# Sums of a GLU unit's first pair in a timed chain, a set's last sums and stores behind it, and other steps for decoding

## The chip, the cores and the metric

One core of one Trainium2 chip runs the whole program. The metric is the device time of one execution in microseconds (us), as the median of several runs. The engines are TensorE (PE, with its weight loads as PEld), VectorE (DVE), ScalarE (ACT), GpSimd (POOL) and SyncE (SP), which issues all DMAs of this kernel.

## What is computed

```python
# attention within chunks of 64 tokens; B, H, S, D = 4, 8, 576, 64
attn = softmax(q_c @ k_c.T / sqrt(D)); x = (attn @ v_c) -> [2304, 512]
# mixture of 4 experts, all of them used, F = 1024
p = domain_probs / domain_probs.sum(-1)
x = sum over e of p[:, e] * (relu(x @ w1[e]) @ w2[e])
# RMSnorm and GLU, F = 1536
xn = x / sqrt(mean(x * x) + 1e-6) * rms_g
out = (silu(xn @ w_gate) * (xn @ w_val)) @ w_out
```

The GLU weights arrive as 64-bit floats and are turned into 32-bit floats on the chip ("decoding").

## The kernel before, in words

**Products.** A 32-bit operand is split into a high part (rounded by a cast on ACT) and a low part (the remainder, a subtraction, mostly on POOL), and a product is three passes of high by high, high by low and low by high. Large products use Strassen's scheme: 7 products in place of 8, with sums of operands before and sums of results after.

**Tiling.** The 2304 tokens are 3 sets of 6 tiles of 128, a set has two blocks of 384 tokens. The program goes through MoE sets 0, 1 and 2 (in the trace about 50 to 800 us, behind an opening piece of attention) and then GLU sets 0, 1 and 2 (801 to 960, 960 to 1117, 1117 to 1282). Attention for set s+1 runs beside MoE set s.

**A GLU unit.** A set has three units (index `k`), a unit two pairs of columns of F (index `fp`). For each pair `hidden` (L766) runs twice, for gate and then for value: seven products a, b, d, c, a, d, c of 6 matmuls each into PSUM tiles `a_ps`, `b_ps`, `c_ps`, `d_ps` (L721). The first product is copied out by ACT (`p`, L774) and the second `a_ps` product may only start after that copy. `gate_use` takes ACT's sigmoid (`sg`, L829) and multiplies on DVE; `val_use` (L850) multiplies by the value (L856), which gives `silu` tiles, and then forms the operand sums `h_s3`, `h_s1`, `h_s2` of the next Strassen product: on POOL for the unit's first pair, on DVE for its second (`late`). `part` (L843) makes the high part of each by a cast on ACT (`hh`, L846) and returns the function that makes the low part on POOL (`hl`).

**The unit's output product.** `outer_strassen` (L926) then multiplies by w_out: seven products (L950) in the order 0, 6, 4, 5, 1, 3, 2, each added by `take` into eight accumulators `out_u2`, `out_c..`, `out_y..`. In a set's last unit (`end`) six closing sums (four on POOL, two on DVE) and the stores of the results (`write`, DMA at L981) stand between these products.

**What sets the order.** The program is written out by one Python pass; each engine executes its instructions in the order in which they were emitted. Beside the main loop stand background generators, the chains of class `Chains` (L73): after each emitted product `work.tick(us)` advances a clock of estimated microseconds, and each chain whose due time has come is stepped; `every` (and `busy` within hidden products) is the spacing of its steps, `pause` a wait on that clock, `force` runs a chain to its end. Chains load weights (`w1_load`, DMA at L298 from `wgv`; w_out by L375 from `wou`, 4 buffers), run attention (`at` = e/sum on POOL, L616, before the transposes `trA` of PE, L526), decode (`decode`, L393; six DVE operations per tile, L405 to L419, and an addition on POOL) and form and store Strassen's weight sums (`prepare`, L429; `store_q`, DMA at L454). Decoding and preparing run from MoE set 1 on:

```python
decode(): every 1.15, busy=3.5;  prepare(): every 1.0
```

A wait at the head of an engine's queue holds up everything behind it, SP's DMA issues included.

Of the kernel before, what the change touches and what calls it, by code (L numbers as in the profile page):

```python
# [18 lines left out]
P = 128  # L19
# [53 lines left out]
class Chains:  # L73
# [78 lines left out]
def fused_kernel(ctx, tc, qkv, probs, w12, wglu, gvec, out):  # L152
# [4 lines left out]
    nc = tc.nc  # L157
# [12 lines left out]
    NB = TPB * P  # L170
# [6 lines left out]
    tp = Slots(tc, ctx, "tp", 32, [P, 512], F32)  # L177
    cp = Slots(tc, ctx, "cp", 8, [P, NB], F32)
# [9 lines left out]
    work = Chains()  # L188
# [11 lines left out]
    sub = lambda eng, o, a, b: eng.tensor_tensor(o, a, b, op=ALU.subtract)  # L200
    add = lambda eng, o, a, b: eng.tensor_tensor(o, a, b, op=ALU.add)  # L201
# [529 lines left out]
    def catch_up():  # L731
        while later:
            later.pop(0)()
# [107 lines left out]
    plain_h, parted = {}, {}  # L841

    def part(fp, n, src):  # L843

        hi, lo = hh.get("hh"), hl.get("hl")
        nc.scalar.copy(hi, src)  # L846
        parted[fp, n] = (hi, lo)
        return lambda: sub(nc.gpsimd, lo, src, hi.bitcast(F32))

    def val_use(fp, late):  # L850
        eng = nc.vector if late else nc.gpsimd

        def use(b, j, ps):
            m = silu.pop((b, j))
            v = m[:, :NB]
            nc.vector.tensor_tensor(v, ps[:, :NB], v, op=ALU.mult)  # L856
            banks.put(ps)
            plain_h[fp, b, j] = m
            at = lambda *bj: plain_h[(fp, *bj)][:, :NB]
            if (b, j) == (1, 1):  # L860
                later.append(part(fp, 0, v))
            elif (b, j) == (0, 1):
                s3, s1 = cp.get("h_s3"), cp.get("h_s1")
                sub(eng, s3, at(1, 1), v)
                add(eng, s1, v, at(0, 0))
                tp.put(plain_h.pop((fp, 0, 1)))
                plain_h[fp, "s1"] = s1
                los = [part(fp, 6, s3), part(fp, 4, s1)]

                def rest():  # L870
                    for lo in los:
                        lo()
                    cp.put(s3)

                later.append(rest)
            elif (b, j) == (1, 0):
                s1, s2 = plain_h.pop((fp, "s1")), cp.get("h_s2")
                sub(eng, s2, s1, at(1, 1))
                cp.put(s1)
                tp.put(plain_h.pop((fp, 1, 1)))  # L880
                lo = part(fp, 5, s2)

                def rest():
                    lo()
                    sub(nc.gpsimd, s2, v, s2)
                    plain_h[fp, "s4"] = s2

                later.append(rest)

        return use  # L890

    acc = {}
# [30 lines left out]
        w2p.put(*w2)  # L923


    def outer_strassen(s, u, fps, end, aside):  # L926

        catch_up()
        w = 2 * P
        if u == 0:  # L930
            for n in ("u2", "c22", "y1", "c11", "c21", "y2", "c12", "y3"):
                acc[n] = tp.get(f"out_{n}")
        spots = {0: (0, 0), 6: (1, 0), 4: (2, 1), 5: (3, 1)}
        big, small, opened = {}, {}, set()

        def mult(n, place, by_tile=False):
            half, y = spots[place]
            half = (0, 1, 1, 0)[half]
            if place not in big:
                big[place] = bank(f"x_{place}")  # L940
                if y not in small:
                    small[y] = bank(f"y_{y}")
            wt = weight(("w2", "glu", s, u, n))
            wv = wt.rearrange("p k (a n) -> p k a n", a=2)
            order = [(q, t) for q in range(UF) for t in range(TPB)]
            for q, t in sorted(order, key=lambda o: o[1]) if by_tile else order:
                ps = big[place] if t < 2 else small[y]
                o = (t if t < 2 else half) * w
                for m, (hx, wi) in enumerate(PASSES):
                    nc.tensor.matmul(  # L950
                        ps[:, o:o + w], parted[fps[q], n][hx][:, t * P:(t + 1) * P], wv[:, q, wi],
                        start=id(ps) not in opened, stop=(n in (1, 2, 3, 5) and (q, m) == (UF - 1, len(PASSES) - 1)),
                        skip_group_check=True,
                    )
                    opened.add(id(ps))
                work.tick(3 * 0.12)
            w2p.put(wt)
            for fp in fps:
                hi, lo = parted.pop((fp, n))
                hh.put(hi)  # L960
                hl.put(lo)

        def take(o, ps, cols=slice(None), first=u == 0):
            if first:
                nc.scalar.copy(acc[o][:, cols], ps[:, cols])
            else:
                add(nc.vector, acc[o][:, cols], ps[:, cols], acc[o][:, cols])
# [7 lines left out]
        low, high = slice(0, w), slice(w, 2 * w)  # L975

        def write(o, cols, b, d, ts):
            i = s * TPS + b * TPB
            for n, t in enumerate(ts):
                c = slice(cols.start + n * w, cols.start + (n + 1) * w)  # L980
                nc.sync.dma_start(out=out[(i + t) * P:(i + t + 1) * P, d * w:(d + 1) * w], in_=acc[o][:, c])  # L981

        mult(0, 0)
        take("u2", big[0])
        more(1, 1, 0)
        aside(0)
        mult(6, 6)
        take("c22", big[6])
        take("y1", small[0])
        more(3, 0, 0)  # L990
        aside(1)
        mult(4, 4)
        take("c22", big[4], first=False)
        more(2, "s4")
        aside(2)
        mult(5, 5)
        take("u2", big[5], first=False)
        take("y1", small[1], first=False)
        banks.put(big[5])
        aside(3)  # L1000
        if end:
            for eng, o, cols, x in (
                (nc.gpsimd, "c21", slice(0, 512), "u2"), (nc.gpsimd, "y2", high, "y1"),
                (nc.vector, "c12", slice(0, 512), "u2"), (nc.vector, "y3", high, "y1"),
                (nc.gpsimd, "c22", slice(0, 512), "u2"), (nc.gpsimd, "y1", high, "y1"),
            ):
                src = acc[x][:, low if x == "y1" else cols]
                add(eng, acc[o][:, cols], acc[o][:, cols], src)
            write("c22", slice(0, 512), 0, 1, (0, 1))
            write("y1", high, 0, 1, (2,))  # L1010
        mult(1, 0)
        take("c11", big[0])
        banks.put(big[0])
        aside(4)
        if end:
            write("c11", slice(0, 512), 1, 0, (0, 1))
        mult(3, 6)
        take("c21", big[6])
        take("y2", small[0])
        banks.put(big[6], small[0])  # L1020
        aside(5)
        if end:
            write("c21", slice(0, 512), 0, 0, (0, 1))
            write("y2", low, 1, 0, (2,))
            write("y2", high, 0, 0, (2,))
        mult(2, 4, True)
        take("c12", big[4])
        take("y3", small[1], high)
        banks.put(big[4], small[1])
        aside(6)  # L1030
        if end:
            write("c12", slice(0, 512), 1, 1, (0, 1))
            write("y3", high, 1, 1, (2,))
            for n in ("u2", "c22", "y1", "c11", "c21", "y2", "c12", "y3"):
                tp.put(acc.pop(n))


    def norm(s):
# [79 lines left out]
    with tc.manual_schedule():  # L1118
# [72 lines left out]
        for kind, s in [(kind, s) for kind in ("moe", "glu") for s in range(NSET)]:  # L1191
            moe = kind == "moe"
            final = not moe and s == NSET - 1
# [5 lines left out]
            for k, (e, fps) in enumerate(plan):  # L1199
                end = k == len(plan) - 1  # L1200
# [8 lines left out]
                    feeding[1] = feeding[3] = 0.8  # L1209
                if moe and s == 1 and k == 0:  # L1210
                    work.add(fetch64())
                    work.add(decode(), 1.15, busy=3.5)
                    work.add(prepare(), 1.0)
                if k == len(plan) - 2 and not final:
                    if ahead is None:
                        ahead = work.add(turn(0 if moe else s + 1), 1.0)
# [40 lines left out]
                if moe:  # L1257
                    outer(fps, w2, flush, aside)
                else:
                    outer_strassen(s, k, fps, end, aside)  # L1260
        work.force(None, lambda: not work.chains)


# [57 lines left out]
```

## Time and profile before

| what | value |
|---|---|
| median of 3 runs | 1280.35 us (1276.58 to 1282.26) |
| profiled execution | 1284.08 us |
| its span | 1282.3 us |
| mean granted TensorE clock | 0.984 of full |
| PE / PEld busy | 1218.4 us (95%) / 1130.6 us (88%) |
| DVE busy | 831.6 us (65%) |
| POOL busy | 714.5 us (56%) |
| ACT busy | 487.5 us (38%) |
| DMA, mean over the span | 233 GB/s |

Busy time of an engine is the time in which one of its instructions runs; PE's 95% leaves about 64 us of the span in which it does nothing. "Granted clock" is the share of full speed that TensorE is given in a stretch: at 0.5 it runs at 1.2 instead of 2.4 GHz and a product takes twice as long while it still counts as busy, so PE's lost time is more than its idle time.

### The profile page before, as it was taken

The page shows a single profiled execution, that of the slowest core. Times are in us where ns is not written, and L with a number is a line of the kernel's source. Part 1 is how long each engine was busy: PE and PEld are TensorE (multiplying, and loading weights), DVE is VectorE, ACT ScalarE, POOL GpSimd, SP SyncE. Part 2 cuts the span into 40 slices and gives each one's busy share as a digit, 9 for nine tenths or more (in the row PEclk, how much of TensorE's full clock was granted, in tenths as well). Part 3 has the DMA queues.
Part 4 walks back from the last instruction along what each step waited for, and adds up shares of the span by engine and source line. Part 5 has one row for each costly group of instructions (what it writes and reads, how often), then busy time and mean ns, then how long its engine had stood idle before and what let it go on. Part 6 is the DMA issues. An engine that isn't in the chain of part 4 may idle for free.

```text
span 1282.3 us, 22321 instructions
## 1 busy us (share of the span) xinstructions
PE 1218.4 (95%) x7740; PEld 1130.6 (88%) x7740; DVE 831.6 (65%) x1450; ACT 487.5 (38%) x1164; POOL 714.5 (56%) x763
## 2 busy tenths in 40 slices
PE   7999999999999999999999999999987999979997
PEld 6878899989999888899899998999986999879997
DVE  5755544475787877887877777645664466644655
ACT  6545433342262344242443333344451432413311
POOL 4797666652575755576755665352464334643434
PEclk9999999999999999999999999999999999989999
DMA  8478555555787997667897786467748658396583
GB/s 266 150 273 276 170 174 195 182 191 197 238 286 261 318 306 246 218 241 254 280 297 273 273 285 245 145 221 264 262 149 276 217 182 288 123 318 204 185 297 115
DMA packets 152898, 299.34 MB, mean 233 GB/s; under 512 B 17745, under 2 KB 22353, under 8 KB 152785
## 3 DMA queue, kind: packets, MB, share of 16 engines
q1 hardware_dynamic: 152784, 297.90, 68.7%
q8 instruction: 62, 1.02, 0.3%
q14 instruction: 52, 0.42, 0.1%
HBM read 227.58 MB, written 70.25 MB: 232 GB/s over the span
## 4 chain that ended last, share of the span: by engine, by line
PE 78%; POOL 9%; DVE 3%; issue 3%; DMA 3%; ACT 2%; SPq 1%; POOLq 0%; DVEq 0%; ACTq 0%
PE o L908 28%; PE d_ps L721 11%; PE a_ps L721 11%; PE c_ps L721 11%; PE x L950 6%; PE b_ps L721 5%; PE y L950 3%; POOL w L200 2%; POOL hl L200 2%; POOL tw L200 1%; DMA w<-wgv 1%; DMA w1m<-w 1%; PE pv L553 1%; POOL h_s L200 1%; POOL at L616 1%
## 5 line engine op out<-in xcount | busy, mean ns | idle before, releaser
L908 PE MATMUL o<-w,hh 128*128 128x512 f32 x1152 | 357.8, 392 | 0.6 <-POOL w L200 0.6
L908 PEld LDWEIGHTS o<-w,hh 128*128 128x128 f32 x1152 | 215.4, 188 | 44.4 <-POOL w L200 1.4
L200 POOL TENSOR_TENSOR w<-r,w 128x512 fp32r<-128x512 f32 (+1 forms) x146 | 164.5, 1135 | 116.0 <-ACT w L360 50.0
L721 PE MATMUL c_ps<-x,w 128*128 128x384 f32 x1080 | 222.3, 344 | 4.2 <-DVE d_ps L201 3.3
L908 PE MATMUL o<-w,hl 128*128 128x512 f32 x576 | 224.8, 390 | 0.0
L721 PE MATMUL a_ps<-x,w 128*128 128x384 f32 x984 | 203.4, 343 | 19.1 <-ACT p L774 19.0
L721 PE MATMUL d_ps<-x,w 128*128 128x384 f32 x984 | 204.6, 345 | 11.9 <-DMA w<-wgv 11.9
L721 PEld LDWEIGHTS c_ps<-x,w 128*128 128x128 f32 x1080 | 193.8, 193 | 6.3 <-DVE d_ps L201 4.7
L721 PEld LDWEIGHTS a_ps<-x,w 128*128 128x128 f32 x984 | 175.3, 192 | 25.4 <-ACT p L774 22.7
L721 PEld LDWEIGHTS d_ps<-x,w 128*128 128x128 f32 x984 | 178.2, 194 | 12.7 <-issue 12.5
L200 POOL TENSOR_TENSOR hl<-silu,hh 128x384 fp32r<-128x384 f32 x54 | 56.6, 1071 | 234.0 <-ACT hh L846 234.0
L1244 DVE SCALAR_TENSOR_TENSOR acc<-o,pr,acc 128x512 f32<-128x512 f32 x126 | 94.3, 749 | 130.9 <-PE o L908 130.8
L908 PEld LDWEIGHTS o<-w,hl 128*128 128x128 f32 x576 | 108.4, 188 | 22.8
L201 POOL TENSOR_TENSOR w<-w,sc 128x512 f32<-128x512 f32 x36 | 46.8, 1299 | 138.2 <-DVE sc L419 131.0
L200 POOL TENSOR_TENSOR w<-tw,w 128x256 fp32r<-128x256 f32 x136 | 112.4, 836 | 4.5 <-ACT w L235 4.5
L201 DVE TENSOR_TENSOR u<-b_ps,p 128x384 f32<-128x384 f32 x82 | 45.4, 554 | 100.3 <-ACT p L774 60.7
L235 ACT CAST w<-tw 128x256 fp32r<-128x256 f32 x136 | 51.7, 406 | 135.0 <-POOL tw L200 131.7
L721 PE MATMUL b_ps<-x,w 128*128 128x384 f32 x492 | 98.7, 336 | 0.0
L950 PE MATMUL x<-w,hh 128*128 128x256 f32 x504 | 95.9, 283 | 0.0
L811 ACT ACTIVATE hh<-d_ps 128x384 fp32r<-128x384 f32 x92 | 45.2, 492 | 127.9 <-DVE d_ps L201 127.9
L200 POOL TENSOR_TENSOR hl<-h_s,hh 128x384 fp32r<-128x384 f32 x72 | 76.8, 1087 | 20.5 <-ACT hh L846 20.5
L774 ACT COPY p<-a_ps 128x384 f32<-128x384 f32 x82 | 39.3, 479 | 126.2 <-PE a_ps L721 126.0
(135 smaller groups left out, 1961.4 us busy)
## 6 DMA issues: line engine op xcount, KB each, us to landing
w<-wgv SPq DMA_DIRECT2D x252, 256.0 KB, 4.5
w<-w1m SPq DMA_DIRECT2D x224, 256.0 KB, 5.3
r<-in_w SPq DMA_DIRECT2D x128, 256.0 KB, 5.0
w<-wou SPq DMA_DIRECT2D x63, 512.0 KB, 6.1
w1m<-w SPq DMA_DIRECT2D x112, 256.0 KB, 2.7
wgv<-w SPq DMA_DIRECT2D x84, 256.0 KB, 4.8
raw<-in_wglu SPq DMA_DIRECT2D x36, 512.0 KB, 4.1
wou<-w SPq DMA_DIRECT2D x42, 256.0 KB, 4.4
```

What stands on the lines that cost most here:

```text
L200: sub = lambda eng, o, a, b: eng.tensor_tensor(o, a, b, op=ALU.subtract)
L201: add = lambda eng, o, a, b: eng.tensor_tensor(o, a, b, op=ALU.add)
L235: nc.scalar.copy(halves(out[n])[:, 0], at[part_of[n]])
L553: nc.tensor.matmul(ps[n][lo:lo + CH, o:o + CH], vt[a][row:row + CH, hp, c, :], aT[a][row:row + CH, q:q + CH], start=True, stop=True,)
L616: nc.gpsimd.tensor_tensor(t.rearrange("p (hp r n) -> p hp r n", hp=HP, r=2)[:, :, h2 ^ a, :], rows(e)[:, a * HP:(a + 1) * HP, :], rs[:, a ...
L721: nc.tensor.matmul(ps[:, :NB], wv[:, wi, k, :], xs[n][:, xi, k, :], start=(first and k == 0 and m == 0), stop=(last and k == KH - 1 and m ...
L774: nc.scalar.copy(p1, v(a))
L811: nc.scalar.activation(hi, src, AF.Relu)
L908: nc.tensor.matmul(ps, hs[fps[k], b, j][hx][:, r * P:(r + 1) * P], w2[2 * k + j][:, wi], start=((k, j, m) == (0, 0, 0)), stop=((k, j, m) = ...
L950: nc.tensor.matmul(ps[:, o:o + w], parted[fps[q], n][hx][:, t * P:(t + 1) * P], wv[:, q, wi], start=id(ps) not in opened, stop=(n in (1, 2 ...
L1244: nc.vector.scalar_tensor_tensor(out=acc[i], in0=ps, scalar=pr[:, i, e:e + 1], in1=acc[i], op0=ALU.mult, op1=ALU.add,)
```

## The change

The core of the diff; `outer_strassen` is now called `second`, and L numbers move by it.

```diff
+    def sums_ahead(fp):
+        at = lambda *bj: plain_h[(fp, *bj)][:, :NB]
+        s3, s1 = cp.get("h_s3"), cp.get("h_s1")
+        sub(nc.gpsimd, s3, at(1, 1), at(0, 1))
+        add(nc.gpsimd, s1, at(0, 1), at(0, 0))
+        tp.put(plain_h.pop((fp, 0, 1)))
+        yield from work.pause(2.8)
+        los = [part(fp, 6, s3), part(fp, 4, s1)]
+        yield from work.pause(1.2)
+        for lo in los:
+            lo()
+        cp.put(s3)
+        while (fp, 1, 0) not in plain_h:
+            yield
+        s2 = cp.get("h_s2")
+        sub(nc.gpsimd, s2, s1, at(1, 1))
...
+        yield from work.pause(1.6)
+        lo = part(fp, 5, s2)
+        yield from work.pause(0.8)
+        lo()
+        sub(nc.gpsimd, s2, at(1, 0), s2)
...
     def val_use(fp, late):
...
+            elif not late:
+                if (b, j) == (0, 1):
+                    summed.append(work.add(sums_ahead(fp)))
...
+    def second(s, u, fps, end, final, aside):
+        for c in summed:
+            if c in work.chains:
+                work.force(c, lambda: c not in work.chains)
...
+        def finish():
+            yield from work.pause(4)
+            for o, y in (("c21", "y2"), ("c12", "y3"), ("c22", "y1")):
+                plus(nc.gpsimd, o)
+                yield from work.pause(1.5)
+                plus(nc.gpsimd, y, high)
+                yield from work.pause(1.5)
+            for args in (
+                ("c11", both, 1, 0, (0, 1)), ("c21", both, 0, 0, (0, 1)), ("c12", both, 1, 1, (0, 1)),
+                ("c22", both, 0, 1, (0, 1)), ("y2", low, 1, 0, (2,)), ("y2", high, 0, 0, (2,)),
+                ("y3", high, 1, 1, (2,)), ("y1", high, 0, 1, (2,)),
+            ):
+                write(*args)
+                yield from work.pause(1)
+            yield from work.pause(5)
+            tp.put(*ac.values())
...
-        if end:
+        if final and end:
...
-            write("c22", slice(0, 512), 0, 1, (0, 1))
-            write("y1", high, 0, 1, (2,))
...
             write("y2", high, 0, 0, (2,))
+            write("c22", both, 0, 1, (0, 1))
+            write("y1", high, 0, 1, (2,))
...
+        elif end:
+            work.add(finish())
...
-                    work.add(decode(), 1.15, busy=3.5)
-                    work.add(prepare(), 1.0)
+                    decoding, preparing = work.add(decode(), 1.15, busy=3.5), work.add(prepare(), 1.0)
+                if moe and (s, k) in ((1, 4), (2, 0)):
+                    decoding[1], decoding[3], preparing[1] = (1.7, 5.0, 1.5) if s == 1 else (1.05, 3.2, 0.9)
```

In words: (1) The sums of a unit's first pair, which were emitted at once inside the value product, are emitted by a chain `sums_ahead` with pauses between sum, cast and remainder; `second` forces the chain to its end before it begins. (2) At the end of GLU sets 0 and 1 the six closing sums, now all on POOL, and the twelve stores are emitted by a chain `finish` behind the unit, beside the next set's first unit, and the eight accumulators stay taken until then. In the last set only the order of the stores changes: those of c22 and y1 stand behind those of c11, c21 and y2. (3) From step 4 of MoE set 1 decoding and preparing take wider steps (1.7, 5.0 and 1.5), and from the start of MoE set 2 closer ones than before (1.05, 3.2 and 0.9).

PE's order of instructions is the same in both kernels. What stands on other engines moves, and the decoding that ended in MoE set 2's last step now ends in GLU set 0's first unit: two tiles' decoding on DVE, about ten POOL operations, casts on ACT and the last seven stores of L454 stand there, two of these stores ahead of the last two w_out loads of that unit.

**ACT, GLU set 0, first unit: end of the first pair's value product and start of the second pair's gate product** (`COPY p` is L774, `hh` the high parts). Before:

```order
L774 COPY p_9891<-a_ps 128x384
L846 CAST hh<-silu 128x384
L846 CAST hh<-h_s_9951 128x384
L846 CAST hh<-h_s_9952 128x384
L846 CAST hh<-h_s_9973 128x384
L774 COPY p_9987<-a_ps 128x384
L829 ACTIVATE sg<-d_ps 128x384
L829 ACTIVATE sg<-a_ps 128x384
L829 ACTIVATE sg<-d_ps 128x384
L829 ACTIVATE sg<-c_ps 128x384
L774 COPY p_10070<-a_ps 128x384
```

Now:

```order
L774 COPY p_9853<-a_ps 128x384
L846 CAST hh<-silu 128x384
L774 COPY p_9938<-a_ps 128x384
L846 CAST hh<-h_s_9923 128x384
L846 CAST hh<-h_s_9924 128x384
L829 ACTIVATE sg<-d_ps 128x384
L829 ACTIVATE sg<-a_ps 128x384
L829 ACTIVATE sg<-d_ps 128x384
L846 CAST hh<-h_s_9994 128x384
L829 ACTIVATE sg<-c_ps 128x384
L774 COPY p_10040<-a_ps 128x384
```

The copy `p` of the next hidden product stands ahead of the two casts of sums, and the third cast stands behind three `sg`.

**SP, end of GLU set 0** (`wgv` are the loads of the next set's first products, `out` the stores). Before:

```order
L375 DMA w_11470<-wou_137 128x1024
L298 DMA w_0_11478<-wgv_0_107 128x512
L298 DMA w_5_11486<-wgv_0_107 128x512
L981 DMA out<-out_c_10148 128x256 x2
L981 DMA out<-out_y_10149 128x256
L298 DMA w_4_11510<-wgv_0_107 128x512
L298 DMA w_6_11521<-wgv_0_107 128x512
L981 DMA out<-out_c_10150 128x256 x2
L298 DMA w_1_11535<-wgv_0_107 128x512
L298 DMA w_2_11543<-wgv_0_107 128x512
L298 DMA w_3_11551<-wgv_0_107 128x512
L981 DMA out<-out_c_10151 128x256 x2
```

Now:

```order
L375 DMA w_11470<-wou_137 128x1024
L298 DMA w_0_11478<-wgv_0_107 128x512
L298 DMA w_5_11486<-wgv_0_107 128x512
L298 DMA w_4_11501<-wgv_0_107 128x512
L298 DMA w_6_11512<-wgv_0_107 128x512
L298 DMA w_1_11524<-wgv_0_107 128x512
L298 DMA w_2_11532<-wgv_0_107 128x512
L298 DMA w_3_11540<-wgv_0_107 128x512
L298 DMA w_0_11555<-wgv_1_108 128x512
L298 DMA w_5_11566<-wgv_1_108 128x512
L298 DMA w_4_11574<-wgv_1_108 128x512
L298 DMA w_6_11588<-wgv_1_108 128x512
```

No store stands between the loads of the next set's first products.

**DVE, end of MoE set 1** (L405 to L419 decode; `s_0`, `s_1` are operand sums of the next set; `u`, `v`, `d_ps` the result sums of the running product). Before:

```order
L405 TENSOR_SCALAR w_6563<-raw 128x512
L1244 SCALAR_TENSOR_TENSOR acc_4079<-o_6556,pr,acc_4079 128x512
L409 SCALAR_TENSOR_TENSOR w_6563<-raw,w_6563 128x512
L413 TENSOR_SCALAR sc<-raw 128x512
L201 TENSOR_TENSOR s_0_6591<-xr 128x384
L200 TENSOR_TENSOR s_0_6593<-s_0_6591,xr 128x384
L201 TENSOR_TENSOR u_6610<-b_ps,p_6596 128x384
L201 TENSOR_TENSOR s_1_6592<-xr 128x384
L201 TENSOR_TENSOR v_6625<-d_ps,u_6610 128x384
L415 SCALAR_TENSOR_TENSOR w_6563<-sc,w_6563 128x512
L200 TENSOR_TENSOR s_1_6594<-s_1_6592,xr 128x384
L200 TENSOR_TENSOR s_0_6637<-xr 128x384
```

Now:

```order
L1304 SCALAR_TENSOR_TENSOR acc_4079<-o_6481,pr,acc_4079 128x512
L419 SCALAR_TENSOR_TENSOR sc<-raw,sc 128x512
L201 TENSOR_TENSOR s_0_6518<-xr 128x384
L200 TENSOR_TENSOR s_0_6520<-s_0_6518,xr 128x384
L201 TENSOR_TENSOR u_6538<-b_ps,p_6523 128x384
L201 TENSOR_TENSOR s_1_6519<-xr 128x384
L201 TENSOR_TENSOR v_6552<-d_ps,u_6538 128x384
L200 TENSOR_TENSOR s_1_6521<-s_1_6519,xr 128x384
L200 TENSOR_TENSOR s_0_6564<-xr 128x384
L201 TENSOR_TENSOR d_ps<-c_ps,v_6552 128x384
```

L405, L409 and L413 of one more tile no longer stand ahead of the sums, nor L415 between `v` and `d_ps`.

## Rows read from the trace of the kernel before

**Rows 1.** The page, part 4: the chain that ended last, by engine.
```profile
PE 78%; POOL 9%; DVE 3%; issue 3%; DMA 3%; ACT 2%; SPq 1%; POOLq 0%; DVEq 0%; ACTq 0%
```

**Rows 2.** Waits of PE, 801 to 1282 us: us in total, times, longest us.
```profile
PE a_ps L721 <- ACT p L774: 17.0, 9, 2.0
PE d_ps L721 <- DMA w<-wgv: 11.9, 2, 6.2
PE x L950 <- POOL hl L200: 4.9, 4, 1.4
PE c_ps L721 <- DMA w<-wgv: 0.8, 1, 0.8
```

**Rows 3.** Timeline of ACT, 829 to 838: start, length, engine, line, operation, idle before.
```profile
833.25 0.52 ACT L846 CAST hh<-h_s 128x384 fp32r<-128x384 f32 x1 [2.66 <-POOL h_s L200]
...
837.11 0.51 ACT L846 CAST hh<-h_s 128x384 fp32r<-128x384 f32 x1 [2.38 <-POOL h_s L200]
837.53 0.47 ACT L774 COPY p<-a_ps 128x384 f32<-128x384 f32 x1
```

**Rows 4.** Timeline of POOL in the same stretch.
```profile
834.15 1.98 POOL L200 TENSOR_TENSOR hl<-h_s,hh 128x384 fp32r<-128x384 f32 x2
836.09 0.99 POOL L200 TENSOR_TENSOR h_s<-h_s,silu 128x384 f32<-128x384 f32 x1
```

**Rows 5.** Timeline of PE in the same stretch.
```profile
834.92 1.21 PE L721 MATMUL c_ps<-x,w 128*128 128x384 f32 x6
838.06 1.32 PE L721 MATMUL a_ps<-x,w 128*128 128x384 f32 x6 [1.93 <-ACT p L774]
839.21 1.20 PE L721 MATMUL d_ps<-x,w 128*128 128x384 f32 x6
840.25 1.20 PE L721 MATMUL c_ps<-x,w 128*128 128x384 f32 x6
```

**Rows 6.** Busy time by windows: window, us, engines, PEclk, DMA share, GB/s.
```profile
933.20:936.80 3.60, 3.56 (x11) 3.56 (x12) 2.23 (x4) 3.57 (x6) 1.70 (x2) 0.53 0.98 346
1246.40:1250.90 4.50, 4.45 (x16) 4.45 (x17) 3.21 (x6) 1.19 (x3) 1.71 (x2) 0.62 0.94 337
971.40:975.20 3.80, 3.68 (x13) 3.42 (x13) 0.63 (x2) 0.00 (x0) 0.00 (x0) 0.61 0.97 276
1128.90:1134.80 5.90, 5.85 (x18) 5.88 (x19) 1.64 (x3) 0.49 (x1) 0.00 (x0) 0.50 1.01 305
```

**Rows 7.** Timeline of SP (its DMA issues), end of GLU set 0.
```profile
952.34 0.90 SPq L298 DMA_DIRECT2D w<-wgv  x2
966.84 0.81 SPq L981 DMA_DIRECT2D out<-out_c  x2
...
968.19 0.94 SPq L298 DMA_DIRECT2D w<-wgv  x2
```

**Rows 8.** Timeline of POOL at the same set end.
```profile
958.86 2.84 POOL L200 TENSOR_TENSOR hl<-h_s,hh 128x384 fp32r<-128x384 f32 x2
...
965.54 1.27 POOL L201 TENSOR_TENSOR out_c<-out_c,out_u 128x512 f32<-128x512 f32 x1
```

**Rows 9.** Timeline of POOL, the same kind of cast remainder inside GLU set 0.
```profile
858.35 1.99 POOL L200 TENSOR_TENSOR hl<-h_s,hh 128x384 fp32r<-128x384 f32 x2
```

**Rows 10.** Waits of PE, 428 to 545 us (attention beside decoding, end of MoE set 1).
```profile
PE trA L526 <- POOL at L616: 4.3, 3, 2.0
PE c_ps L721 <- DVE d_ps L201: 2.2, 1, 2.2
```

**Rows 11.** Timeline of DVE at the end of MoE set 1.
```profile
527.39 1.55 DVE L405 TENSOR_SCALAR w<-raw 128x512 uint32<-128x512 uint32 x1
...
536.68 0.56 DVE L201 TENSOR_TENSOR d_ps<-c_ps,v 128x384 f32<-128x384 f32 x1
```

**Rows 12.** Timeline of SP, end of the program.
```profile
1274.15 0.81 SPq L981 DMA_DIRECT2D out<-out_c  x2
...
1279.51 0.40 SPq L981 DMA_DIRECT2D out<-out_y  x1
```

More of the change, by code (lines that the diff above doesn't have):

```diff
@@ L848, in part @@
         return lambda: sub(nc.gpsimd, lo, src, hi.bitcast(F32))
+    def sums_ahead(fp):
[14 more added lines that the diff above has]
+        sub(nc.gpsimd, s2, s1, at(1, 1))
+        cp.put(s1)
+        tp.put(plain_h.pop((fp, 1, 1)))
+        yield from work.pause(1.6)
[3 more added lines that the diff above has]
+        sub(nc.gpsimd, s2, at(1, 0), s2)
+        plain_h[fp, "s4"] = s2
+    summed = []
     def val_use(fp, late):
-        eng = nc.vector if late else nc.gpsimd
         def use(b, j, ps):
@@ L861, in use @@
                 later.append(part(fp, 0, v))
+            elif not late:
+                if (b, j) == (0, 1):
+                    summed.append(work.add(sums_ahead(fp)))
             elif (b, j) == (0, 1):
                 s3, s1 = cp.get("h_s3"), cp.get("h_s1")
-                sub(eng, s3, at(1, 1), v)
-                add(eng, s1, v, at(0, 0))
+                sub(nc.vector, s3, at(1, 1), v)
+                add(nc.vector, s1, v, at(0, 0))
                 tp.put(plain_h.pop((fp, 0, 1)))
@@ L877, in use @@
                 s1, s2 = plain_h.pop((fp, "s1")), cp.get("h_s2")
-                sub(eng, s2, s1, at(1, 1))
+                sub(nc.vector, s2, s1, at(1, 1))
                 cp.put(s1)
@@ L923, in outer, with mult @@
         w2p.put(*w2)
-    def outer_strassen(s, u, fps, end, aside):
+    SUMS = ("u2", "c22", "y1", "c11", "c21", "y2", "c12", "y3")
+    def second(s, u, fps, end, final, aside):
+        w = 2 * P
+        low, high, both = slice(0, w), slice(w, 2 * w), slice(0, 2 * w)
+        for c in summed:
+            if c in work.chains:
+                work.force(c, lambda: c not in work.chains)
+        summed.clear()
         catch_up()
-        w = 2 * P
         if u == 0:
-            for n in ("u2", "c22", "y1", "c11", "c21", "y2", "c12", "y3"):
+            for n in SUMS:
                 acc[n] = tp.get(f"out_{n}")
-        spots = {0: (0, 0), 6: (1, 0), 4: (2, 1), 5: (3, 1)}
+        ac = {n: acc[n] for n in SUMS}
         big, small, opened = {}, {}, set()
-        def mult(n, place, by_tile=False):
-            half, y = spots[place]
-            half = (0, 1, 1, 0)[half]
+        def mult(n, place, y, half, by_tile=False):
             if place not in big:
@@ L961, in mult, with take @@
                 hl.put(lo)
-        def take(o, ps, cols=slice(None), first=u == 0):
+        def take(o, ps, cols=both, first=u == 0):
             if first:
-                nc.scalar.copy(acc[o][:, cols], ps[:, cols])
+                nc.scalar.copy(ac[o][:, cols], ps[:, cols])
             else:
-                add(nc.vector, acc[o][:, cols], ps[:, cols], acc[o][:, cols])
+                add(nc.vector, ac[o][:, cols], ps[:, cols], ac[o][:, cols])
         def more(n, *names):
@@ L973, in more, with plus @@
                 (cp if names == ("s4",) else tp).put(t)
-        low, high = slice(0, w), slice(w, 2 * w)
+        def plus(eng, o, cols=both):
+            src = ac["u2"] if cols is both else ac["y1"][:, low]
+            add(eng, ac[o][:, cols], ac[o][:, cols], src)
         def write(o, cols, b, d, ts):
@@ L980, in write @@
                 c = slice(cols.start + n * w, cols.start + (n + 1) * w)
-                nc.sync.dma_start(out=out[(i + t) * P:(i + t + 1) * P, d * w:(d + 1) * w], in_=acc[o][:, c])
-        mult(0, 0)
+                nc.sync.dma_start(out=out[(i + t) * P:(i + t + 1) * P, d * w:(d + 1) * w], in_=ac[o][:, c])
+        def finish():
[14 more added lines that the diff above has]
+            tp.put(*ac.values())
+        mult(0, 0, 0, 0)
         take("u2", big[0])
@@ L986, in outer_strassen @@
         aside(0)
-        mult(6, 6)
+        mult(6, 6, 0, 1)
         take("c22", big[6])
@@ L991, in outer_strassen @@
         aside(1)
-        mult(4, 4)
+        mult(4, 4, 1, 1)
         take("c22", big[4], first=False)
@@ L995, in outer_strassen @@
         aside(2)
-        mult(5, 5)
+        mult(5, 5, 1, 0)
         take("u2", big[5], first=False)
@@ L1000, in outer_strassen @@
         aside(3)
-        if end:
[L1002 to L1008, printed above, removed]
-            write("c22", slice(0, 512), 0, 1, (0, 1))
-            write("y1", high, 0, 1, (2,))
-        mult(1, 0)
+        if final and end:
+            plus(nc.gpsimd, "c21")
+            plus(nc.gpsimd, "y2", high)
+            plus(nc.vector, "c12")
+            plus(nc.vector, "y3", high)
+            plus(nc.gpsimd, "c22")
+            plus(nc.gpsimd, "y1", high)
+        mult(1, 0, 0, 0)
         take("c11", big[0])
@@ L1014, in outer_strassen @@
         aside(4)
-        if end:
-            write("c11", slice(0, 512), 1, 0, (0, 1))
-        mult(3, 6)
+        if final and end:
+            write("c11", both, 1, 0, (0, 1))
+        mult(3, 6, 0, 1)
         take("c21", big[6])
@@ L1021, in outer_strassen @@
         aside(5)
-        if end:
-            write("c21", slice(0, 512), 0, 0, (0, 1))
+        if final and end:
+            write("c21", both, 0, 0, (0, 1))
             write("y2", low, 1, 0, (2,))
             write("y2", high, 0, 0, (2,))
-        mult(2, 4, True)
+            write("c22", both, 0, 1, (0, 1))
+            write("y1", high, 0, 1, (2,))
+        mult(2, 4, 1, 1, True)
         take("c12", big[4])
@@ L1031, in outer_strassen @@
         if end:
-            write("c12", slice(0, 512), 1, 1, (0, 1))
+            for n in SUMS:
+                acc.pop(n)
+        if final and end:
+            write("c12", both, 1, 1, (0, 1))
             write("y3", high, 1, 1, (2,))
-            for n in ("u2", "c22", "y1", "c11", "c21", "y2", "c12", "y3"):
-                tp.put(acc.pop(n))
+            tp.put(*ac.values())
+        elif end:
+            work.add(finish())
     def norm(s):
@@ L1259, in fused_kernel @@
                 else:
-                    outer_strassen(s, k, fps, end, aside)
+                    second(s, k, fps, end, final, aside)
         work.force(None, lambda: not work.chains)
```

## The prediction, made before the changed kernel ran

> **What bounds the kernel now.** I read the page first: PE is busy for 95% of the span and 78% of the chain that ended last is PE's own work [rows 1], so a gain must come from PE's idle time, from the stretches where its clock is down, or from the ends. Second I read PE's waits over the GLU sets [rows 2]: 17.0 us for ACT's copy `p`, nine times (once per unit), 11.9 + 0.8 us for weight loads, and 4.9 us for remainders from POOL. The reader is to see that each is a small number of long waits. Third, the timelines around one of each, to see what the waited-for engine was doing [rows 3 to 5, 7, 8], and fourth the granted clock behind them [rows 6]: after six of the nine waits for `p`, and after both long load waits, TensorE is given its lower level, 1.2 in place of 2.4 GHz, for some microseconds. Last, PE's waits where attention runs beside decoding [rows 10].
>
> **Part 1, the chain of sums.** ACT idles 2.38 us in front of the third cast of a sum because POOL makes two remainders (1.98 us) and then the sum h_s2, which ends at 837.08 [rows 3, 4]. The copy `p` is queued behind that cast and starts at 837.53. The product it copies was done long before: c_ps starts at 834.92, products follow each other at 1.04 us (839.21 to 840.25), so the a_ps product three places ahead ended by about 833. PE then starts 3.14 us after c_ps in place of 1.04, and the next one 1.15 us later: 2.21 us lost for 1.93 us of idle time [rows 5].
> Over nine units: 17.0 us idle; nine restarts at about 0.2, 1.8; and six low-clock stretches. The first costs 3.6 x (1 - 0.53) = 1.7 us, the last 4.5 x (1 - 0.62) = 1.7 us [rows 6], so six cost 10.2. Together **29.0 us**. In the new order `p` stands ahead of the casts, and none of the three has to be there for the products of the next hidden pass; the chain is forced before the output product, two passes of seven products (14.6 us) later. Nothing is added: the same sums, casts and remainders, three of each, on the same engines.
> What is late next: the third cast now stands ahead of the last `sg` and the following `p`. Without the wait the gate's last product would start at about 838.0 (834.92 + 3 x 1.04), its end and that `sg` come at about 839 to 840, while h_s2 was ready at 837.08. It has 2 to 3 us to spare, so I cost it at nothing; this cover gone is a rival below.
>
> **Part 2, closing sums and stores.** At the end of GLU set 0 SP issues two loads, then a store of c22 that cannot go before 966.84, when POOL's sum of 965.54 + 1.27 is done, and only then the third load, at 968.19 [rows 7, 8]. PE waits for that one. SP could have sent it at 953.3, 15 us earlier, so the whole wait should go. Twice, with one small follower: 11.9 + 0.8 = 12.7 us idle [rows 2], 3.8 x 0.39 = 1.5 and 5.9 x 0.50 = 2.95 us of low clock [rows 6], and 1 us for the restarts: **18 us**. Added: nothing but two additions that go from DVE to POOL. Past SP move twelve stores, which now stand among the w_out loads of the next unit, needed after its four passes of seven products (29 us); past POOL six sums of up to 1.27 us, beside a first pair whose remainders are needed only at the output product. Both I cost at nothing, covered by that distance.
> PE also waits for remainders at these ends, 4.9 us in four waits [rows 2]. POOL needed 2.84 us for two of them there, beside DVE's closing sums, against 1.99 us for two elsewhere [rows 8, 9]. With those sums gone from DVE, up to 0.85 us per end would return; other DVE sums remain beside it, so I take half, **0.9 us** for both.
> The Trainium skill, page "SBUF — State Buffer", section "Who interferes with whom", says that a DVE operation with both inputs in SBUF blocks a GpSimd operation that reads SBUF; by that alone the sum would gain 1.7 instead of 0.9, and POOL's six moved sums would in turn hold up such DVE operations in the next unit. The two rows fit it; no row shows the second half.
> The end: twelve stores go out from 1274.15 to 1279.91, 0.48 us each, all behind the one that waits for POOL's c22 [rows 12]. Now six of them stand ahead and can go while POOL works: 2.9 us if all six are out by 1274.15; the sums they wait for end shortly before that time, so I take **2.5 us** (0 to 2.9).
>
> **Part 3, decoding.** Where attention runs beside it PE waits 4.3 us for POOL's `at`, whose sums on DVE are queued among decode operations, and 2.2 us at the end of MoE set 1 for DVE's d_ps [rows 10], where decode operations such as L405 (1.55 us) fill DVE up to the d_ps of 536.68 [rows 11]. With clock and restarts by the ratio of part 1 (29.0 / 17.0 = 1.7) these 6.5 us are 11 us. In the new order some of the decode operations are gone from these places, not all, so I take two thirds, 7. The same work is then closer together in MoE set 2, with no long PE wait there before; I take 2 us against it. Net **5 us** gained. Bounds: at best 9 (most of the 11, nothing given back); at worst 4 lost, if set 2 gets two waits like the 2.2 us one.
> The rest of the decoding falls into GLU set 0's first unit. There two stores that wait for POOL stand ahead of w_out loads. The nearest row for a load held behind such a store is part 2's: 5.9 us per wait. Nothing lost is the other bound. Only two loads with four buffers are concerned, so I take **2.5 us** lost, between 0 and 6.
> **New short waits.** When nine waits go, engines meet that were not late before. The nearest rows are waits of about 0.8 us (the last line of [rows 2]); four of them make **3 us**, between 0 and 8.
>
> **The sum.** -29.0 - 18 - 0.9 - 2.5 - 5 + 2.5 + 3 = -49.9 us. Against the profiled execution's 1284.08 this gives 1234.2; that execution stands 3.7 us over the median of the runs shown, so the median should be 1230.5, I say **1230 us**. The cost bounds: all good ends together give 1230 - 4 - 2.5 - 3 = 1220, bad ends of the single terms 1234 to 1239.
>
> **Rivals.**
> (a) The clock does not come back. 10.2 + 4.5 = 14.7 us of the sum are low clock [rows 6]. For the forecast speaks that each drop follows a long wait; against it, that three of nine waits of the same 1.9 us brought none, so the wait alone does not decide. Then 1245; half of it, 1237. 10%.
> (b) Decoding takes instead of giving: -4 for +5 and 6 for 2.5, so 1242.5. For it: DVE and POOL are fullest in that stretch, and the loads of GLU set 0's first unit now share SP with late stores. 17%.
> (c) The set-end load wait stays: SP's third load has another condition, such as a buffer that comes free late, and part 2 does not do what it says: 1230 + 18 = 1248. Against it, the third load goes at 968.19, as soon as the stores ahead of it are issued [rows 7], so nothing else held it by then. 6%.
> (d) Slower: ACT stops at the third cast. If POOL makes h_s2 late, the last `sg` and the next `p` wait behind it, and PE as now, one pass later. It begins when h_s2 is over 2 to 3 us later than at 837.08 and needs (50 + 6.4) / 9 = 6.3 us per unit to be slower than before, so POOL 9 us late in all nine units; two units have moved sums in front, of about 6 us, seven have none. Half of it would end at no change, about 1280 (3%); all of it at 1290 (2%).
>
> **How the numbers follow.** The forecast, with its own range of 1222 to 1238, has 62%; (a) 10, (b) 17, (c) 6, (d) 5. A difference of 0.5% (6.4 us) is about what a measurement of this kernel can tell. The forecast, (a), (b) and (c) all lie far below 1274: faster 0.95; no change 0.03; slower 0.02. The range goes from **1219** (the good ends, and 1 us of scatter) to **1246**, which takes in (a) and (b) and leaves out (c), (d) and the tails.
>
> **What would show it.** Right: no wait of PE for ACT's `p` in the GLU sets and no clock below 1 behind it; all weight loads of the next set issued within a few microseconds of the first, without a store between, and no PE wait for `wgv`; the last stores issued by about 1277.5 on the old scale; fewer waits on `at` and d_ps in 428 to 545. Wrong: ACT idle in front of a cast of h_s with `sg` or `p` behind it; PE waiting for `wou` in GLU set 0; PE waits for DVE or POOL in MoE set 2; a low clock in GLU stretches without a wait ahead.

## The result and the profile after

The changed kernel took **1231.3 us** (median of 4 runs, 1229.9 to 1232.23) against 1281.3 us for the kernel before (4 runs, 1276.58 to 1283.67): a ratio of 0.9613, 95% interval 0.9584 to 0.9643. The prediction said 1230. The profiled execution of the changed kernel took 1229.9 us, that of the kernel before 1284.08; their spans differ by 54.5 us.

The changed kernel's page, its parts 1 and 4:

```profile
span 1227.8 us, 22297 instructions
...
PE 1199.7 (98%) x7740; PEld 1116.7 (91%) x7740; DVE 823.5 (67%) x1446; ACT 487.6 (40%) x1164; POOL 721.6 (59%) x767
...
PE 84%; POOL 5%; DVE 4%; DMA 3%; issue 2%; ACT 1%; SPq 0%; POOLq 0%; DVEq 0%; ACTq 0%
```

Against the table of before, PE is busy 18.7 us less (1218.4 to 1199.7) with the same 7740 instructions, and idle 35.8 us less (63.9 to 28.1). The first number is mostly low clock that no longer comes, the second idle time; together they are the 54.5 us between the spans. PE's own share of the chain rose from 78% [rows 1] to 84%.

PE's waits over the GLU sets, to be read beside [rows 2]:

```profile
PE x L986 <- POOL hl L200: 4.8, 5, 1.6
PE x L986 <- DMA w<-wou: 0.7, 1, 0.7
```

The nine waits for ACT's `p` and the three for `wgv` are gone. What stays is the wait for POOL's remainders, 4.8 us where it was 4.9, and a new one of 0.7 us for a w_out load. The 4.8 us are not the same waits as the 4.9: at the two set ends PE waits 3.7 us in place of 4.9, and 1.1 us are a new wait in GLU set 0's first unit (see "Decoding" below).

**The chain of sums.** ACT and then PE, the changed kernel, at the place of [rows 3, 5] (in ACT's rows first the cast of h_s1, then the third cast and what stands behind it):

```profile
826.81 0.52 ACT L846 CAST hh<-h_s 128x384 fp32r<-128x384 f32 x1 [0.76 <-POOL h_s L201]
...
831.41 0.51 ACT L846 CAST hh<-h_s 128x384 fp32r<-128x384 f32 x1
832.00 0.49 ACT L829 ACTIVATE sg<-c_ps 128x384 f32<-128x384 f32 x1
832.49 0.48 ACT L774 COPY p<-a_ps 128x384 f32<-128x384 f32 x1
```

```profile
828.08 1.20 PE L721 MATMUL a_ps<-x,w 128*128 128x384 f32 x6
829.12 1.20 PE L721 MATMUL d_ps<-x,w 128*128 128x384 f32 x6
...
832.24 1.20 PE L721 MATMUL b_ps<-x,w 128*128 128x384 f32 x6
```

The products follow at 1.04 us; the third cast (831.41) waits for nothing, and the last `sg` and the next `p` come right behind it.

**The set end.** SP's issues at the end of GLU set 0, where [rows 7] had a store between the second and the third load:

```profile
938.85 27.64 SPq L298 DMA_DIRECT2D w<-wgv  x28
966.54 0.90 SPq L375 DMA_DIRECT2D w<-wou  x2
967.54 1.07 SPq L1019 DMA_DIRECT2D out<-out_c  x2
```

All 28 loads go in one row from 938.85 on, and the first store comes 28.7 us later. POOL at the end of set 1, and two windows behind PE's waits at the ends of sets 1 and 0 (columns as in [rows 6]):

```profile
1075.45 5.32 POOL L200 TENSOR_TENSOR hl<-silu,hh 128x384 fp32r<-128x384 f32 x4
1080.73 2.69 POOL L200 TENSOR_TENSOR x<-s,x 128x384 fp32r<-128x384 f32 x2
1083.38 1.95 POOL L200 TENSOR_TENSOR hl<-h_s,hh 128x384 fp32r<-128x384 f32 x2
```

```profile
1087.00:1090.00 3.00, 3.00 (x13) 3.00 (x12) 1.52 (x3) 0.35 (x1) 3.00 (x4) 0.53 0.29 107
949.00:952.00 3.00, 3.00 (x21) 3.00 (x20) 2.62 (x4) 0.48 (x1) 3.00 (x3) 1.00 0.62 199
```

The two remainders that PE waits for (1083.38) take 1.95 us now, in place of 2.84 [rows 8], but they stand behind four remainders of 5.32 us and two of the next set's operand, 2.69 us. Behind the wait at the end of set 1 the clock falls to 0.53; at the end of set 0 it does not. The order on POOL is that of before. PE's two waits at the end of GLU set 0, before:

```profile
960.08 0.39 PE L950 MATMUL x<-w,hl 128*128 128x256 f32 x1 [1.42 <-POOL hl L200]
...
961.75 0.38 PE L950 MATMUL x<-w,hl 128*128 128x256 f32 x1 [1.04 <-POOL hl L200]
```

Now:

```profile
946.72 0.39 PE L986 MATMUL x<-w,hl 128*128 128x256 f32 x1 [1.56 <-POOL hl L200]
...
947.68 0.39 PE L986 MATMUL x<-w,hl 128*128 128x256 f32 x1 [0.34 <-POOL hl L200]
```

All of what is gained is in the second wait.

**Decoding.** PE's waits in 428 to 545, then in 545 to 800, the second also of the kernel before:

```profile
PE trA L526 <- POOL at L616: 2.8, 2, 1.7
PE c_ps L721 <- DVE d_ps L201: 0.7, 1, 0.7
PE pv L553 <- ACT aT L531: 0.5, 1, 0.5
```

```profile
PE a_ps L721 <- ACT p L774: 0.8, 1, 0.8
PE c_ps L721 <- DVE d_ps L201: 0.3, 1, 0.3
```

Before:

```profile
PE a_ps L721 <- ACT p L774: 1.4, 2, 0.8
PE c_ps L721 <- DVE d_ps L201: 1.1, 1, 1.1
```

and SP in the first unit of GLU set 0:

```profile
841.61 0.38 SPq L375 DMA_DIRECT2D w<-wou  x1
842.09 5.14 SPq L454 DMA_DIRECT2D wou<-w  x2
847.32 0.87 SPq L375 DMA_DIRECT2D w<-wou  x2
```

The wait at the end of MoE set 1 fell from 2.2 to 0.7 us, those for `at` from 4.3 to 2.8 us [rows 10], and the short ones in MoE set 2 from 2.5 to 1.1 us in all. In the GLU unit two late stores (842.09) hold SP until the w_out loads of 847.32; PE waits 0.7 us for them, and 1.1 us for a remainder that POOL makes behind late preparing.

**The end.**

```profile
1218.34 3.05 SPq L1019 DMA_DIRECT2D out<-out_c  x4
...
1222.48 0.90 SPq L1019 DMA_DIRECT2D out<-out_c  x2
...
1224.95 0.41 SPq L1019 DMA_DIRECT2D out<-out_y  x1
```

The last store is issued at 1224.95, 3.5 us behind PE's last product (1221.4); before it was 5.7 us (1279.51 against 1273.8). The runs below repeat this: with the old order of the last stores (part 1 alone, only the stores later) it is 5.7 us, with the new order (part 2 alone) 3.5.

PE's idle time adds up from these rows: 17.0 us for `p`, 12.7 for loads, 1.2 for remainders at the set ends, 2.2 at the end, 2.5 in 428 to 545 (6.5 to 4.0) and 1.4 in MoE set 2, less 1.8 of new waits in GLU set 0's first unit. That is 35.2 of the 35.8 us.

### The profile page after: what moved, and what is told of

The parts are those of the page before. It is cut to its first block, busy times and chain, and to the rows that moved or that the text cites. A ratio compares the mean times of both kernels' runs of the same rounds, so it can differ in the third digit from the quotient of the medians.

```text
span 1227.8 us, 22297 instructions
## 1 busy us (share of the span) xinstructions
PE 1199.7 (98%) x7740; PEld 1116.7 (91%) x7740; DVE 823.5 (67%) x1446; ACT 487.6 (40%) x1164; POOL 721.6 (59%) x767
## 4 chain that ended last, share of the span: by engine, by line
PE 84%; POOL 5%; DVE 4%; DMA 3%; issue 2%; ACT 1%; SPq 0%; POOLq 0%; DVEq 0%; ACTq 0%
PE o L937 29%; PE c_ps L721 13%; PE d_ps L721 12%; PE a_ps L721 12%; PE b_ps L721 6%; PE x L986 6%; PE y L986 3%; POOL w L200 1%; POOL hl L200 1%; POOL tw L200 1%; DMA v<-in_qkv 1%; PE pv L553 1%; DMA w1m<-w 1%; PE xT L1163 1%; DMA r<-in_w 1%
## 5 line engine op out<-in xcount | busy, mean ns | idle before, releaser
L200 POOL TENSOR_TENSOR w<-r,w 128x512 fp32r<-128x512 f32 (+1 forms) x146 | 167.4, 1153 | 120.0 <-ACT w L360 46.0
L721 PE MATMUL c_ps<-x,w 128*128 128x384 f32 x1080 | 216.7, 338 | 1.0 <-DVE d_ps L201 0.9
L721 PE MATMUL a_ps<-x,w 128*128 128x384 f32 x984 | 199.2, 338 | 1.2 <-ACT p L774 1.2
L721 PE MATMUL d_ps<-x,w 128*128 128x384 f32 x984 | 198.0, 337 | 0.0
L721 PEld LDWEIGHTS c_ps<-x,w 128*128 128x128 f32 x1080 | 188.5, 188 | 2.4 <-DVE d_ps L201 2.0
L721 PEld LDWEIGHTS d_ps<-x,w 128*128 128x128 f32 x984 | 172.5, 188 | 0.1
L774 ACT COPY p<-a_ps 128x384 f32<-128x384 f32 x82 | 39.4, 481 | 147.2 <-PE a_ps L721 147.2
```

The lines of the kernel that those rows point to most:

```text
L721: nc.tensor.matmul(ps[:, :NB], wv[:, wi, k, :], xs[n][:, xi, k, :], start=(first and k == 0 and m == 0), stop=(last and k == KH - 1 and m ...
L774: nc.scalar.copy(p1, v(a))
```

## The experiments

Nine kernels. "Before" in each stands for the kernel before on the same chip. The changed kernel was not run again beside them, so a run that starts from it is compared with it by the ratios to the kernel before.

**Part 1 alone** on the kernel before: `sums_ahead`, `val_use` and the forcing of the chain.

```diff
+    def sums_ahead(fp):
...
+                    summed.append(work.add(sums_ahead(fp)))
```

> Part 1 alone on the kernel before. Theory (the waits are separate and each takes its low-clock stretch with it): the nine waits of PE for ACT's p go, 17 us idle and 12 us of clock and restarts, so 29 us: about 1252 us against 1281. Rival (the clock falls whatever the waits do): 17 to 19 us, about 1263. Rival (the three parts only pay together, since the set ends come late anyway): under 12 us, 1270 or more.

Measured: 1254.31 us against 1280.44, ratio 0.9801 (0.9777 to 0.9825): 26 us. PE's waits over the GLU sets:

```profile
PE d_ps L721 <- DMA w<-wgv: 9.8, 2, 6.2
PE x L983 <- POOL hl L200: 5.0, 4, 1.5
```

The wait for `p` is gone in all nine units, and the set ends still wait (9.8 us for `wgv` in place of 12.7, 5.0 for remainders). So the first theory holds, at 26 us (22 to 28.6 by the interval).

**Part 2 alone** on the kernel before: `second` with `finish`.

```diff
+        def finish():
...
-                    outer_strassen(s, k, fps, end, aside)
+                    second(s, k, fps, end, final, aside)
```

> Part 2 alone on the kernel before (closing sums and stores of GLU sets 0 and 1 behind the unit, other order of the last stores). Theory: 18 us of set-end load waits with their clock and 2.5 us at the end, less about 1 us of longer waits for POOL's remainders: about 1261.5 us against 1281. Rival (the clock is not given back): 15 us, 1266. Rival (most of it hangs on part 1): under 8 us, 1273 or more.

Measured: 1263.11 us against 1280.44, ratio 0.9874 (0.9844 to 0.9904): 17.3 us.

```profile
PE a_ps L721 <- ACT p L774: 18.4, 9, 2.6
PE x L953 <- POOL hl L200: 3.7, 4, 1.5
```

No wait for `wgv` is left. The nine waits for `p` are slightly longer (18.4 us in place of 17.0): the two in the first units of sets 1 and 2, beside the sums that POOL now makes there, are 2.6 us each in place of 1.9. The waits for remainders are shorter, 3.7 us in place of 4.9.

**Part 3 alone** on the kernel before.

```diff
+                if moe and (s, k) in ((1, 4), (2, 0)):
+                    decoding[1], decoding[3], preparing[1] = (1.7, 5.0, 1.5) if s == 1 else (1.05, 3.2, 0.9)
```

> Part 3 alone on the kernel before (steps of decoding and preparing). Theory: 8 us gained up to MoE set 2, about 2 us lost in GLU set 0's first unit: 6 us, about 1275 us against 1281. Rival (what it gains comes from a shorter GLU stretch, that is from parts 1 and 2): no change, 1281. Rival (the late decoding costs more without part 1, since ACT's queue is blocked there): slower, 1283 to 1288.

Measured: 1278.39 us against 1280.44, ratio 0.9984 (0.9970 to 0.9998): 2 us (0.3 to 3.8 by the interval), between the theory's 6 and no change. In its trace PE's waits in 428 to 545 are as short as in the changed kernel (at the end of MoE set 1 0.7 us), and in GLU set 0's first unit it waits 1.0 us for a remainder and 0.9 us for a w_out load, where the kernel before waited for neither.

**Part 3 undone** in the changed kernel.

```diff
-                    decoding[1], decoding[3], preparing[1] = (1.7, 5.0, 1.5) if s == 1 else (1.05, 3.2, 0.9)
+                    work.add(decode(), 1.15, busy=3.5)
+                    work.add(prepare(), 1.0)
```

> The changed kernel with the decoding and preparing steps of the kernel before (part 3 undone). Theory (part 3 is worth the 8 us that the trace shows up to the end of MoE set 2, less about 2 us in GLU set 0's first unit): about 1237 us against the changed kernel's 1231. Rival (part 3 alone brought 2 us, and no more beside the others): 1233. Rival (it is worth more beside the others, what the three parts alone leave open): 1235 to 1239.

Measured: 1234.28 us against 1281.78, ratio 0.9632 (0.9601 to 0.9663). That is 3.0 us over the changed kernel's median; the two ratios' intervals overlap. The medians put part 3 at 2 to 3 us in either company. The second line, 1233, is nearest, but the difference is not clear of noise, so the theory's 6 and the rival by which it pays more beside the others are unlikely and not excluded. PE's waits in 428 to 545 are those of [rows 10]: 4.3 us for `at` and 2.2 us for d_ps. But the longest of those for `at` and the window behind it read here

```profile
439.98 0.66 PE L526 MATMUL trA<-ident,at 128*128 128x128 f32 x4 [2.03 <-POOL at L616]
...
440.00:444.60 4.60, 4.60 (x24) 3.87 (x25) 3.28 (x5) 1.38 (x3) 4.60 (x7) 1.00 0.94 358
```

and in the kernel before

```profile
440.79 0.66 PE L526 MATMUL trA<-ident,at 128*128 128x128 f32 x4 [2.03 <-POOL at L616]
...
440.80:445.40 4.60, 4.60 (x18) 3.77 (x18) 2.59 (x4) 1.48 (x3) 4.60 (x7) 0.63 0.83 314
```

The same wait is followed by a clock of 0.63 in one execution and 1.00 in another, and none of the parts in which the two kernels differ has begun by then. Part of what a single trace shows as part 3's gain is this.

**Only the third cast behind `p`**, on the kernel before.

```diff
-                lo = part(fp, 5, s2)
+                lo = part(fp, 5, s2) if late else None
 
                 def rest():
-                    lo()
+                    (lo or part(fp, 5, s2))()
```

> On the kernel before, only the third cast (that of h_s2) of a unit's first pair is emitted behind the next copy p; sums, the other two casts and everything else stay at their places. Theory (p stands behind a cast that waits for POOL's third sum, the first two casts are early enough): nearly all of part 1, 25 to 29 us, about 1254 us. Rival (the first two casts hold p as well): a wait of some tenths to 1 us stays in each unit, 10 to 20 us gained, 1261 to 1271. Rival (DVE's u or a bank, not p, ends the wait): no gain, 1281.

Measured: 1256.91 us against 1280.44, ratio 0.9817 (0.9792 to 0.9841): 23.5 us, 2.6 us short of part 1 alone, with overlapping intervals.

```profile
PE d_ps L721 <- DMA w<-wgv: 9.0, 2, 4.6
...
PE a_ps L721 <- ACT p L774: 1.1, 1, 1.1
```

```profile
834.44 0.51 ACT L846 CAST hh<-h_s 128x384 fp32r<-128x384 f32 x1 [0.46 <-POOL h_s L201]
834.86 0.47 ACT L774 COPY p<-a_ps 128x384 f32<-128x384 f32 x1
837.36 0.51 ACT L846 CAST hh<-h_s 128x384 fp32r<-128x384 f32 x1 [2.03 <-POOL h_s L200]
```

`p` starts at 834.86, right behind the second cast, and one wait of nine is left (1.1 us). So nearly all of part 1 was one cast at the wrong place in ACT's queue; what the timed spacing of the other sums adds, 2.6 us, is not clear of noise.

**Only the stores later**, on the kernel before: the stores of GLU sets 0 and 1 go into a chain behind the unit, the closing sums stay on their engines and places.

```diff
+        def stores(*args):
+            write(*args) if final else kept_back.append(args)
+
+        def finish():
+            yield from work.pause(13)
+            for args in kept_back:
+                write(*args)
+                yield from work.pause(1)
...
-            write("c22", slice(0, 512), 0, 1, (0, 1))
+            stores("c22", slice(0, 512), 0, 1, (0, 1))
```

> On the kernel before, at the ends of GLU sets 0 and 1 only the stores are emitted later, behind the unit; the six closing sums keep their places and engines, and the last set is as before. Theory (the load wait comes from SP's order alone): the two waits for wgv go, 18 us with their clock, about 1262 us against 1280, and the waits for POOL's remainders stay at 4.9 us. Rival (the sums on POOL at this place matter too): under 14 us gained, and a load wait of 1 us or more stays.

Measured: 1267.29 us against 1281.78, ratio 0.9890 (0.9862 to 0.9917): 14.5 us (10.6 to 17.7 by the interval).

```profile
PE a_ps L721 <- ACT p L774: 17.2, 9, 2.1
PE x L950 <- POOL hl L200: 5.0, 4, 1.4
PE d_ps L721 <- POOL x L200: 0.5, 2, 0.3
```

The load waits are gone with the stores alone; two short waits of 0.3 us and less for POOL's operand appear. The mechanism is SP's order, as the theory says, and the size is under its 18 us. With the 2.2 us at the end that the changed order of the last stores brings, 14.5 comes to 16.7, near part 2's 17.3: for moving the sums off this place there is less than 1 us, within the intervals nothing. The traces show two effects of it that about cancel: the waits for remainders are 1.3 us shorter in part 2 alone (3.7 for 5.0) and those for `p` 1.2 us longer (18.4 for 17.2).

**One step further: the next operand behind the remainders**, on the changed kernel.

```diff
         more(3, 0, 0)
-        aside(1)
         mult(4, 4, 1, 1)
         take("c22", big[4], first=False)
         more(2, "s4")
+        aside(1)
         aside(2)
```

> The changed kernel; at a set's end the remainder of the next set's second operand on POOL is made behind the remainders for the last output product instead of ahead of them. Theory (what still waits at set ends is queue order on POOL): the two waits of 1.5 and 0.3 us each go, with the low clock behind the second one: 4 to 6 us, about 1226 us. Rival (POOL is held by DVE's sums there and is late in any order): under 1 us, 1231. Rival (the next set's second product now waits for that operand): 1231 to 1235.

Measured: **1224.75 us** against 1281.78, ratio 0.9558 (0.9535 to 0.9581), 6.5 us under the changed kernel's median and, by the intervals, faster than it.

```profile
PE x L986 <- POOL hl L200: 1.6, 3, 1.1
PE x L986 <- DMA w<-wou: 0.6, 1, 0.6
```

Of 4.8 us of waits 1.6 are left, 1.1 of them in GLU set 0's first unit; at the set ends 3.7 us became 0.5. With the low clock behind the wait at the end of set 1, some 1.7 us that no longer come, this accounts for 5.0 of the 5.2 us by which the two traces' spans differ. So the order on POOL set what was left of the wait at the set ends.

**And the late decoding earlier**, on the run before this one.

```diff
-                    ... else (1.05, 3.2, 0.9)
+                    ... else (1.0, 3.0, 0.85)
```

> The run before this one, and decoding and preparing in MoE set 2 at 1.0, 3.0 and 0.85 in place of 1.05, 3.2 and 0.9, so that all of it ends ahead of GLU set 0. Theory (the late decoding costs the 2.3 us of waits for POOL's remainder and for a w_out load in that unit): 2 us under the run before, about 1224 us. Rival (closer steps bring new waits in MoE set 2): the same as the run before, or 1 to 3 us over it.

Measured: 1224.98 us, ratio 0.9560 (0.9538 to 0.9583): no change. The two waits in GLU set 0's first unit are gone, and PE's waits in 545 to 800 now read

```profile
PE c_ps L721 <- DVE d_ps L201: 1.9, 2, 1.5
```

where the run before it had 0.3 us for d_ps (and 0.8 for `p`, which is 0.3 here): the GLU unit gives 1.7 us, and MoE set 2 takes 1.1 of it back in waits.

**DVE's operation moved as well**, on the run with the operand behind the remainders.

```diff
         more(1, 1, 0)
-        aside(0)
...
+        aside(0)
         aside(1)
```

> As the run with the operand behind the last remainders, and the first operand's remainder on DVE (both inputs in SBUF) is moved behind them too, so that DVE has no such operation beside POOL's four remainders at a set's end. Theory (DVE operations with two SBUF inputs hold POOL there): those four take about 4.0 us as inside a set, in place of 5.3, and the last short waits of 0.2 us go; the time changes by under 1 us from 1224.75. Rival (POOL's remainders are longer there for another reason): they stay at 5.3 us.

Measured: 1223.2 us against 1281.29, ratio 0.9556 (0.9526 to 0.9587): the same time as without it. PE's short waits at the set ends are gone. POOL's four remainders, and the DVE operations with both inputs in SBUF that now stand beside their end:

```profile
936.90 4.67 POOL L200 TENSOR_TENSOR hl<-silu,hh 128x384 fp32r<-128x384 f32 x4
```

```profile
938.88 1.80 DVE L200 TENSOR_TENSOR x<-xr,x 128x768 fp32r<-128x768 f32 x1 [0.90 <-ACT x L706]
940.61 2.67 DVE L200 TENSOR_TENSOR x<-s,x 128x384 fp32r<-128x384 f32 x2
```

4.67 us in place of 5.3, not 4.0: half of the theory. But the edit did not clear the place: the DVE operations start at 938.88, half-way through the four, and run beside them for 2.7 us. In the run that it starts from, where they stand at 937.12 and 940.46, it was 2.7 us as well. What changed is who lost time: POOL 0.7 us in place of 1.4, while the DVE operations take 1.80 us in place of 1.62 and 2.67 in place of 1.85. So this run does not say what POOL needs there without them.

## Why the prediction was right

**Part 1, 29.0 us.** Right in mechanism, shown by two runs: 26 us for all of the part, 23.5 for the third cast alone. (A restart was put at 0.2 us where its own row gives 2.21 - 1.93 = 0.28; over nine units that is under 1 us.) The third cast has the room that was worked out (it waits for nothing at 831.41). Rival (d) did not come.

**Part 2, 18 us.** Right in mechanism: the stores alone take the wait away. The term was over-sized: 14.5 us with the stores alone. Some 5 of the 18 were low clock and restarts put down to the load wait; without it, a stretch of low clock comes behind the remainders' wait just ahead, as at the end of set 1 in the trace after. So of rival (a), that the clock does not come back, a small piece came true.

**Remainders at the set ends, 0.9 us.** Right in kind, a little small: the two remainders fell from 2.84 to 1.95 us, and PE's waits at the two set ends from 4.9 to 3.7 us in all, 1.2 us less. Part 2 alone shows the same 3.7 us; with the stores alone, which leave the sums on DVE, it is 5.0. What the step did not look at is the queue of the instruction waited for: four remainders and two of the next set's operand stand ahead on POOL. The run that turns this order takes another 3.3 us of wait, and 6.5 us of time. The Trainium skill, page "SBUF — State Buffer", section "Who interferes with whom", says that a DVE instruction with two SBUF inputs contends with a GpSimd instruction that reads SBUF, and the trace of after agrees in kind (the prediction reckoned 1.7 us by that rule alone, and 1.2 were measured): POOL's four remainders take 5.32 us where such DVE operations run beside them for 2.7 us, and 3.95 us in GLU set 0's first unit, where the DVE operations beside them read one input from PSUM:

```profile
846.84 3.95 POOL L200 TENSOR_TENSOR hl<-silu,hh 128x384 fp32r<-128x384 f32 x4
```

**The end, 2.5 us.** Measured from PE's last product to the last issue: 2.2 us, in each pair of kernels with the old and the new order.

**Part 3, 5 us gained and 2.5 lost.** The net of 2.5 us is what the runs show (2 alone, 3 when undone), but its pieces came out otherwise. The waits at the places named fell by 3.0 of 6.5 us, where two thirds were reckoned, and a new one of 0.5 us stands beside them; MoE set 2, put at 2 us lost, waits 1.4 us less; GLU set 0's first unit has 1.8 us of new waits, 0.7 for a w_out load behind two stores and 1.1 for a remainder of POOL, which was not foreseen. The 1.7 by which the idle time was multiplied held a low-clock stretch that the same wait does not always bring.

**New short waits, 3 us.** Not found: outside that one unit the GLU sets show no new wait. The whole term was wrong.

**The sum.** The sum said 49.9 us and the medians differ by 50.0; that they agree so closely is luck. By the medians parts 1 and 2 alone brought 7 us less than reckoned (26.1 for 29.0, 17.3 for 21.4); the 3 us of new waits that did not come stand against that. The three parts alone add to 45.5 us, and the change brought 4.5 more. The traces account for 1.9 us of it: the waits for `p` that part 1 removes are 1.4 us longer in part 2 alone and 0.5 us longer in part 3 alone. With intervals of 2 to 4 us to either side on each, the rest is left open.

## What to carry to other kernels

An instruction that waits costs what stands behind it on its engine's queue: one cast that waits for another engine's sum cost some 25 us, a store ahead of loads, at two places, some 15 us, and moving them behind the urgent work took no work away. Read for a wait not only what ended it but the whole queue ahead of the instruction waited for; there lay the next 6.5 us. Work that runs beside the main products can be spread or pressed together, but in the one run that pressed it further together (1224.98 against 1224.75 us) one stage took back what the other gave.

## What the runs showed of the hardware

The same PE wait (2.03 us, in a stretch where the kernels are alike) was followed by a granted clock of 0.63 in one execution, that is by the lower level of 1.2 GHz for most of the 4.6 us window, and of 1.00 in another. Six traces hold this wait at this place with nothing changed ahead of it: the kernel before, part 1 alone, only the third cast and only the stores show the drop (0.66 to 0.68 in 441 to 446), part 2 alone and part 3 undone do not (1.00). In the trace of before, six of nine waits of 1.5 to 2.0 us were followed by it. So a low-clock stretch found behind one wait in one trace is a chance and not a price: in part 2 alone and with the stores alone such stretches came behind other waits.
